# A loop over the heads, four fixed load buffers and padded queries from one masked product, in an attention kernel for one token

## The chip, the core and the metric

The kernel runs on one core of a Trainium2 chip. The metric is the time of one execution on the device in microseconds (us). The kernel before is given by the median of three runs, and one further execution was profiled.

## What is computed

One decoding step for 8 sequences. The input row of each is normalised, projected to 32 query heads of 128 numbers and attends over a cache of 8192 keys and values for each of 8 key-value heads (four query heads share one). The output projection, the input itself and a small mixer over the normalised row are added.

```
xn = _layernorm(x, axis=-1)
q = (x @ wq).reshape(B, Sq, Hq, Dh)          # x is xn here
scores = jnp.einsum("bhqd,bhkd->bhqk", q, k) * (Dh ** -0.5)
p = _softmax(scores, axis=-1)
o = jnp.einsum("bhqk,bhkd->bhqd", p, v)      # then @ wo
...
h = _layernorm(x, axis=-1)                   # mixer, x is xn
u = _gelu(jnp.einsum("bsd,sf->bdf", h, w1) + b1)
y = jnp.einsum("bdf,fs->bds", u, w2) + b2
return x + _A_ref(xn, ...) + _B_ref(xn, ...)
```

The sizes: B = 8 sequences, 8 key-value heads, 8192 keys of 128 numbers, all float32. A key tile and a value tile of one pair (head, sequence) have 4 MB each; there are 64 pairs, so 512 MB of cache, and 8 MB each of wq and wo.

## The kernel before, in words

The program is written out in full: 64 slots, one for each pair, with i = 8h + b, and the order of every engine's instructions is the order of the text (`manual_schedule`). The 4 MB tiles lie in a ring of five buffers (`ring`, name `raw`) that keys, values, wq and the last part of wo share. The order of the loads is a list: K0, K1, V0, K2, V1, K3, V2 and so on. `load_next` (L67 to L77) issues the next one on SyncE's queue. Two ring buffers are first filled with the halves of wq, and three loads stand behind them; two more are issued after the query projection has read wq. From then on `qk` (L224) and `pv` (L266) each issue one load when their last product is in the text, and the load waits until the ring buffer that it takes has been read.

A slot i goes like this:

- `qk(i)` (L228): 32 score products from the key tile and the padded queries `W`, into one PSUM bank of 128 x 512. Before it, VectorE has turned the key tile in place with four 32 x 32-block transposes (`turn`, L218). The four transposes for pair i+1 are spread over slot i.
- `sm_max`, `sm_bias`, `sm_exp` (L238, L243, L246, L252): the row maximum, its spreading over the heads by a product with the identity, a masked minimum that gives the bias, and the exponential on ScalarE, which also writes the row sums into `LR`.
- `sm_place` (L259, L261): a permuting product and a transpose that give `PT`, the weights as the value product needs them.
- `pv(i-1)` (L272): 32 value products of the pair before; `o_pick` and `o_place` (L283 to L294) gather its output.
- two steps of the mixer (L346 to L348), ScalarE's gelu and two operations of GpSimd.

At b = 0 a new head begins. The slot then also has `mx_begin` (L336, L338: a row of the normalised input spread to all partitions), `o_sums` (L311, L313), `o_scale` (L316) and `o_project` (L326, L328) of the head before. `LR`, `W` and `OTS` exist twice, for even and odd heads. `q_place` (L211) copies the queries of a whole head into the zeroed tile `W` in eight copies of 32 partitions, spread over slots 3 to 6 of the head before. `load_wo` loads 1 MB of wo for each of the first six heads in slot 2; the last two parts come behind the last value tile in a ring buffer, and `o_project(h - 1, h)` (L326) treats both heads at the end.

The last two pairs are written out by hand in an order of their own, with the last key and value tile loaded in pieces.

Of the kernel before, what the change touches and what calls it, by code (L numbers as in the profile page):

```python
# [28 lines left out]
RING = 5  # L29
PAD = 16  # L30
# [3 lines left out]
def attn_mixer_kernel(ctx: ExitStack, tc: tile.TileContext, x, kc, vc, wq, wo, w1, b1, w2, b2, out):  # L34
    nc = tc.nc
    const = ctx.enter_context(tc.tile_pool(name="const", bufs=1))
    ring = ctx.enter_context(tc.tile_pool(name="ring", bufs=RING))
# [3 lines left out]
    ps_s = ctx.enter_context(tc.tile_pool(name="ps_s", bufs=2, space=PSUM))  # L41
    ps_o = ctx.enter_context(tc.tile_pool(name="ps_o", bufs=2, space=PSUM))
    ps_h = ctx.enter_context(tc.tile_pool(name="ps_h", bufs=2, space=PSUM))
    ps_m = ctx.enter_context(tc.tile_pool(name="ps_m", bufs=2, space=PSUM))
    ctx.enter_context(tc.manual_schedule())

    def misc():
        return ps_m.tile([P, 512], F32, name="misc")
# [8 lines left out]
    order.sort(key=lambda o: o[0])  # L57
    order.reverse()
    WQ = []

    def load_wq():
        for a in range(2):
            t = ring.tile([P, NT, DH], F32, name="raw")
            t = t.rearrange("p (c n) d -> p c (n d)", c=NC // 2)
            nc.sync.dma_start(t, wq.rearrange("(p c) n -> p c n", c=NC)[:, a * NC // 2:(a + 1) * NC // 2, :])
            WQ.extend(t[:, c, :] for c in range(NC // 2))

    def load_next():
        if order:
            _, src, to, i = order.pop()  # L70
            h, b = divmod(i, B)
            t = ring.tile([P, NT, DH], F32, name="raw")
            rows = src[b, h].rearrange("(p t) d -> p t d", p=P)
            at = 0
            for n in (NT // 4,) * 4 if to is KR and i in (0, N_IT - 1) else (NT // 2, NT // 4, NT // 8, NT // 8) if not order else (NT,):
                nc.sync.dma_start(t[:, at:at + n, :], rows[:, at:at + n, :])
                at += n  # L77
            to[i] = t
        elif HKV - 1 not in wos:
            t = ring.tile([P, NT, DH], F32, name="raw")  # L80
            t = t.rearrange("p (h r c) d -> p h r (c d)", h=4, r=REP)
            for h in (HKV - 2, HKV - 1):
                rows = wo[h * REP * DH:(h + 1) * REP * DH, :].rearrange("(r p) n -> p r n", p=P)
                wos[h] = t[:, h % 2]
                for r in (slice(0, REP),) if h < HKV - 1 else (slice(0, REP - 1), slice(REP - 1, REP)):
                    nc.sync.dma_start(wos[h][:, r, :], rows[:, r, :])

    wos = {}

    def load_wo(h):  # L90
        t = one.tile([P, REP, D], F32, name="wo")
        nc.sync.dma_start(t, wo[h * REP * DH:(h + 1) * REP * DH, :].rearrange("(r p) n -> p r n", p=P))
        wos[h] = t
# [10 lines left out]
    for _ in range(RING - 2):  # L104
        load_next()
# [16 lines left out]
    nc.vector.tensor_scalar(hmask, ohw, 1.0, 3.0e38, op0=ALU.subtract, op1=ALU.mult)  # L122
# [13 lines left out]
    BO = BS * (B - 1)  # L136
    bsel = const.tile([P, BO + Q], F32, name="bsel")
    nc.vector.memset(bsel, 0.0)
    nc.vector.memset(bsel[:, BO:BO + 1], 1.0)
# [3 lines left out]
    W, OTS, LR = [], [], []  # L143
    for k in range(2):
        t = const.tile([P, B, NB, Q], F32, name=f"w{k}")
        nc.gpsimd.memset(t, 0.0)
        W.append(t)
        t = const.tile([P, REP, Q], F32, name=f"ot{k}")
        nc.vector.memset(t, 0.0)
        OTS.append(t)  # L150
        LR.append(const.tile([P, B], F32, name=f"lr{k}"))

# [25 lines left out]
    QT = const.tile([P, HKV, NB, REP, B], F32, name="qt")  # L178

    def q_project():  # L180
        hw = HKV // 2
        for a in range(2):
            m = ps_s.tile([P, 512], F32, name="s")
# [8 lines left out]
            mt = ps_o.tile([P, 512], F32, name="o")  # L192
# [9 lines left out]
            for h in range(hw):  # L202
                nc.vector.tensor_copy(QT[:, a * hw + h],
                                      mq.rearrange("p (j h x) -> p h j x", j=NB, h=hw)[:, h].rearrange("p j (r b) -> p j r b", r=REP))
        WQ.clear()

    def q_place(h, i):
        s = slice(i * Q, (i + 1) * Q)
        for k in range(2):
            o = (2 * i + k) * REP  # L210
            nc.vector.tensor_copy(W[h % 2][s, :, :, o:o + REP], QT[s, h].rearrange("p j r b -> p b j r"))  # L211

    def turn(i, a, w=NT // 4):
        if i < N_IT:
            t = KR[i][:, a:a + w, :].rearrange("p t d -> p (t d)")
            nc.vector.transpose(t, t)  # L218

    S = {}  # L220

    def qk(i):
        h, b = divmod(i, B)
        S[i] = ps_s.tile([P, 512], F32, name="s")  # L224
        kt = KR.pop(i).rearrange("p (u g) d -> p g u d", g=NG)
        for j in range(NB):
            for g in range(NG):
                nc.tensor.matmul(S[i][g * Q:(g + 1) * Q, :], W[h % 2][:, b, j, :], kt[:, g, :, j * Q:(j + 1) * Q],  # L228
                                 start=(j == 0), stop=(j == NB - 1))
        load_next()  # L230
# [3 lines left out]
    st = {}  # L234

    def sm_max(i):
        mr = work.tile([P, 1], F32, name="mr")
# [142 lines left out]
    def slot(i):  # L380
# [6 lines left out]
        if i:  # L387
            pv(i - 1)
# [85 lines left out]
```

## Time and profile before

| | |
|---|---|
| median of 3 runs | 1296.01 us (1295.83 to 1296.05) |
| the profiled execution | 1296.24 us, of which 1294.3 us lie between its first and last instruction (the span) |
| busy share of the span | TensorE 61%, VectorE 62%, ScalarE 22%, GpSimd 18% |
| moved by the DMA engines | 554.50 MB, mean 428 GB/s |
| chain of work that ended last | DMA 60%, TensorE 21%, VectorE 12%, issue 4%, ScalarE 3% |

In the rows below PE is TensorE (PEld its weight loads), DVE VectorE, ACT ScalarE, POOL GpSimd, SP SyncE, whose queue issues nearly all loads. A row of a timeline has the start in us, the duration in us, the engine, the line, the operation, the tile written and the tiles read, the shapes and the count; in square brackets stand the idle time before it and what ended that. Equal neighbours are merged into one row with their count. A row of the page's groups has the total busy time in us, the mean of one in ns, and the idle time before the group with its main cause. A row of DMA issues has the size of one and the median time in us from issue to landing.

### The profile page before, as it was taken

The page shows a single profiled execution, that of the slowest core. Times are in us where ns is not written, and L with a number is a line of the kernel's source. Part 1 is how long each engine was busy: PE and PEld are TensorE (multiplying, and loading weights), DVE is VectorE, ACT ScalarE, POOL GpSimd, SP SyncE. Part 2 cuts the span into 40 slices and gives each one's busy share as a digit, 9 for nine tenths or more (in the row PEclk, how much of TensorE's full clock was granted, in tenths as well). Part 3 has the DMA queues.
Part 4 walks back from the last instruction along what each step waited for, and adds up shares of the span by engine and source line. Part 5 has one row for each costly group of instructions (what it writes and reads, how often), then busy time and mean ns, then how long its engine had stood idle before and what let it go on. Part 6 is the DMA issues. An engine that isn't in the chain of part 4 may idle for free.

```text
span 1294.3 us, 12448 instructions
## 1 busy us (share of the span) xinstructions
PE 783.8 (61%) x5178; PEld 260.0 (20%) x5178; DVE 805.3 (62%) x834; ACT 289.4 (22%) x365; POOL 231.2 (18%) x244
## 2 busy tenths in 40 slices
PE   3376657646566556666476565575655854656657
PEld 2121112111121112211122111131111311121112
DVE  2676575575765755756656647557576566666574
ACT  0032221221212312213112222022130231213320
POOL 1022211212112111122112121121220221203310
PEclk9688777877777777787777776867868777768779
DMA  9999999999999999999999999999999999999997
GB/s 405 434 426 430 427 436 435 429 430 436 430 429 436 431 431 433 433 431 431 432 432 434 433 428 433 435 430 432 434 429 432 436 431 428 436 434 432 429 431 322
DMA packets 24491, 554.50 MB, mean 428 GB/s; under 512 B 2508, under 2 KB 2540, under 8 KB 6900
## 3 DMA queue, kind: packets, MB, share of 16 engines
q1 hardware_dynamic: 24292, 553.67, 99.5%
q8 instruction: 41, 0.67, 0.2%
q14 instruction: 14, 0.11, 0.0%
q10 hardware_dynamic: 16, 0.02, 0.0%
q0 software_dynamic: 128, 0.02, 0.0%
HBM read 553.69 MB, written 0.02 MB: 428 GB/s over the span
## 4 chain that ended last, share of the span: by engine, by line
DMA 60%; PE 21%; DVE 12%; issue 4%; ACT 3%; SPq 0%; ACTq 0%; DVEq 0%
DMA raw<-in_A_k_cache_dram 57%; DVE raw L218 10%; PE s L228 9%; PE o L272 5%; PE misc L259 3%; DMA raw<-in_A_wo_dram 2%; ACT L252 2%; DMA raw<-in_A_wq_dram 2%; DVE mr L238 1%; ACT t2k L252 1%; PE s L188 1%; PE misc L336 1%; PE misc L326 1%; PE misc L311 0%; DVE t2k L283 0%
## 5 line engine op out<-in xcount | busy, mean ns | idle before, releaser
L218 DVE STREAM_TRANSPOSE raw<-raw 128x2048 f32<-128x2048 f32 x256 | 581.9, 2293 | 346.8 <-DMA raw<-in_A_k_cache_dram 346.7
L228 PE MATMUL s<-raw,w 128*32 128x512 f32 x2048 | 315.3, 770 | 16.9 <-issue 11.8
L347 POOL TENSOR_SCALAR g<-g,w2t 128x512 f32<-128x512 f32 x112 | 77.7, 694 | 898.4 <-ACT g L346 898.4
L272 PE MATMUL o<-raw,pt 128*32 128x512 f32 x2048 | 231.4, 592 | 1.9 <-DMA raw<-in_A_v_cache_dram 1.1
L294 PE MATMUL mh<-sel,ob 128*128 128x4 f32 x126 | 35.0, 348 | 311.4 <-DVE ob L287 311.4
L252 ACT ACT_TABLE_LOAD x55 | 70.6, 1283 | 589.8 <-DVE nb L246 589.7
L348 POOL TENSOR_TENSOR macc<-macc,g 128x512 f32<-128x512 f32 x112 | 144.4, 1290 | 9.3
L259 PE MATMUL misc<-t2k,perm 128*128 128x512 f32 x128 | 124.7, 1075 | 14.4 <-ACT t2k L252 14.4
L228 PEld LDWEIGHTS s<-raw,w 128*32 128x32 f32 x2048 | 75.7, 141 | 269.0 <-issue 253.0
L346 ACT ACTIVATE g<-hb,b1t,w1t 128x512 f32<-128x512 f32 x112 | 91.0, 813 | 128.9 <-POOL macc L348 128.2
L243 PE MATMUL misc<-ident,mr 128*128 128x128 f32 x128 | 33.1, 342 | 134.0 <-DVE mr L238 134.0
L294 PEld LDWEIGHTS mh<-sel,ob 128*128 128x128 f32 x126 | 29.5, 291 | 325.4 <-DVE ob L287 324.5
L272 PEld LDWEIGHTS o<-raw,pt 128*32 128x32 f32 x2048 | 62.3, 110 | 158.1 <-issue 155.0
L252 ACT ACTIVATE t2k<-s,nb 128x512 f32<-128x512 f32 x64 | 44.0, 687 | 193.6 <-DVE nb L246 193.0
L261 DVE STREAM_TRANSPOSE pt<-misc 128x512 f32<-128x512 f32 x64 | 45.6, 712 | 42.4 <-PE misc L259 42.4
L346 ACT ACT_TABLE_LOAD x54 | 69.3, 1283 | 1.4
L243 PEld LDWEIGHTS misc<-ident,mr 128*128 128x128 f32 x128 | 20.2, 198 | 190.8 <-DVE mr L238 182.4
L238 DVE TENSOR_REDUCE mr<-s 128x1 f32<-128x512 f32 x64 | 42.1, 658 | 19.8 <-PE s L228 19.8
L283 DVE TENSOR_TENSOR t2k<-o,dm 128x512 f32<-128x512 f32 x63 | 43.1, 685 | 0.0
L211 DVE COPY w<-qt 32x128 f32<-32x128 f32 x64 | 37.0, 616 | 0.7
L259 PEld LDWEIGHTS misc<-t2k,perm 128*128 128x128 f32 x128 | 30.5, 296 | 20.3 <-ACT t2k L252 18.7
L286 DVE TENSOR_TENSOR ob<-t2k 128x256 f32<-128x256 f32 x63 | 26.8, 425 | 2.2
(75 smaller groups left out, 200.0 us busy)
## 6 DMA issues: line engine op xcount, KB each, us to landing
raw<-in_A_v_cache_dram SPq DMA_DIRECT2D x63, 4096.0 KB, 31.8
raw<-in_A_k_cache_dram SPq DMA_DIRECT2D x62, 4096.0 KB, 38.2
raw<-in_A_wq_dram SPq DMA_DIRECT2D x2, 4096.0 KB, 16.9
raw<-in_A_k_cache_dram SPq DMA_DIRECT2D x8, 1024.0 KB, 30.3
wo<-in_A_wo_dram SPq DMA_DIRECT2D x6, 1024.0 KB, 40.2
raw<-in_A_v_cache_dram SPq DMA_DIRECT2D x1, 2048.0 KB, 33.9
raw<-in_A_v_cache_dram SPq DMA_DIRECT2D x1, 1024.0 KB, 36.0
raw<-in_A_v_cache_dram SPq DMA_DIRECT2D x2, 512.0 KB, 26.8
```

Of the source, the lines that this page charges most:

```text
L218: nc.vector.transpose(t, t)
L228: nc.tensor.matmul(S[i][g * Q:(g + 1) * Q, :], W[h % 2][:, b, j, :], kt[:, g, :, j * Q:(j + 1) * Q], start=(j == 0), stop=(j == NB - 1))
L238: nc.vector.tensor_reduce(mr, S[i], AX.X, ALU.max)
L243: nc.tensor.matmul(m[:, :P], st[i].to_broadcast([P, P]), ident, start=True, stop=True)
L252: nc.scalar.activation(p, S.pop(i), AF.Exp, bias=st[i], scale=SCALE, accum_out=LR[h % 2][:, b:b + 1])
L259: nc.tensor.matmul(m, perm, st.pop(i), start=True, stop=True)
L261: nc.vector.transpose(PT[i], m)
L272: nc.tensor.matmul(O[i][c * Q:(c + 1) * Q, :], PT[i][:, u * Q:(u + 1) * Q], VR[i][:, u * NG:(u + 1) * NG, :].rearrange("p t d -> p (t d)") ...
L294: nc.tensor.matmul(MH[h][:, b * REP:(b + 1) * REP], OB.pop(i)[:, :DH], sel, start=True, stop=True)
L346: nc.scalar.activation(g, hb, AF.Gelu_apprx_tanh, bias=b1t[:, j:j + 1], scale=w1t[:, j:j + 1])
L347: nc.gpsimd.tensor_scalar(g, g, w2t[:, j:j + 1], 1.0, op0=ALU.mult, op1=ALU.mult)
L348: nc.gpsimd.tensor_add(acc, acc, g)
```

## The change

- **Loop.** Slot (0, 0) stands ahead of a loop. The loop has seven rounds; a round h holds the slots (h, 1) to (h, 7) and (h+1, 0). It has marks between stages after the slots 2, 4 and 6, and waits for the stage before on four engines after the slots 1, 3, 5 and 7. The slots (7, 1) to (7, 5) and the hand-written end follow it. There is a `prologue_barrier` ahead of slot (0, 0) and an `epilogue_barrier` at the end.
- **Buffers.** The ring becomes two key tiles and two value tiles, taken by the parity of b. wq is loaded into the two value tiles. In slot (h, b) the load of K for two pairs later stands right behind `qk(b)`, and the load of V for the next pair right behind `pv(b - 1)`. Two key loads are issued at the start, the first value load after the query projection. All other tiles and PSUM banks become fixed too, many of them single where they were double (`LR`, `OTS`, the head's output bank).
- **Queries.** `W` holds one pair instead of a head, twice. One VectorE product with a mask of zeros and ones, `imask`, writes it whole, one slot ahead.
- **Head change.** With `LR` single, `o_sums` moves ahead of `sm_exp`; `o_scale` and `o_project` move ahead of `mx_begin`, whose selecting column and that of `mx_end` are copied by two small products that read at an address from a register.
- **Smaller edits.** `sm_bias` is an addition and a minimum in place of one combined operation. GpSimd's scaling by w2 becomes a product with a broadcast; the first step of a head writes the sum directly, without the clearing and the addition. wo for the heads 0 to 6 is loaded in slot 2, and only head 7's part comes behind the last value tile.

```diff
-    KR, VR = {}, {}
-    order = []
-    for i in range(N_IT):
-        order.append((2 * i, kc, KR, i))
-        order.append((2 * i + 2.5, vc, VR, i))
...
+    K = [ring.tile([P, NT, DH], F32, name=f"k{k}") for k in range(2)]
+    V = [ring.tile([P, NT, DH], F32, name=f"v{k}") for k in range(2)]
...
+    def load(to, src, h, b, pieces=(NT,)):
+        rows = src[b, h, :, :].rearrange("(p t) d -> p t d", p=P)
+        at = 0
+        for n in pieces:
+            nc.sync.dma_start(to[b % 2][:, at:at + n, :], rows[:, at:at + n, :])
+            at += n
...
-    for _ in range(RING - 2):
-        load_next()
+    load(K, kc, 0, 0, (NT // 4,) * 4)
+    load(K, kc, 0, 1)
...
+    def q_place(h, b):
+        nc.vector.tensor_tensor(W[b % 2].rearrange("p j (x r) -> p j x r", r=REP),
+                                QT[:, h, b].unsqueeze(2).to_broadcast([P, NB, 2 * NB, REP]),
+                                imask.rearrange("p i k -> p (i k)").unsqueeze(1).unsqueeze(3).to_broadcast([P, NB, 2 * NB, REP]), ALU.mult)
...
+    def sm_bias():
         m = misc()
+        nc.tensor.matmul(m[:, :P], MR.to_broadcast([P, P]), nident, start=True, stop=True)
+        nc.vector.tensor_tensor(SQ, m[:, :P], hmask, ALU.add)
+        nc.vector.tensor_reduce(NBIAS, SQ, AX.X, ALU.min)
...
+    def mx_begin(h):
+        m = MI[2]
+        nc.vector.tensor_tensor(BM, ident[:B, bass.ds(h, 1)], ident[:B, bass.ds(h, 1)], ALU.mult)
+        nc.vector.tensor_tensor(BW, bsel[:, h, :], bsel[:, h, :], ALU.mult)
+        nc.tensor.matmul(m, BM.to_broadcast([B, P]), hn, start=True, stop=True)
+        nc.scalar.copy(HB, m)
+
+    def mx_step(j):
+        nc.scalar.activation(G, HB, AF.Gelu_apprx_tanh, bias=b1t[:, j:j + 1], scale=w1t[:, j:j + 1])
+        nc.gpsimd.tensor_tensor(G if j else ACC, G, w2t[:, j:j + 1].to_broadcast([P, D]), ALU.mult)
+        if j:
+            nc.gpsimd.tensor_add(ACC, ACC, G)
...
     q_project()
-    load_next()
-    load_next()
-    for i in range(NB):
-        q_place(0, i)
+    load(V, vc, 0, 0)
+    q_place(0, 0)
...
+    def slot(h, b, last=False, first=False):
+
+        q_place(*after(h, b, 1))
+        qk(b)
+        load(K, kc, *after(h, b, 2), (NT // 4,) * 4 if last and b == B - 3 else (NT,))
+        turn(b + 1, 0)
+        sm_max(b)
+        turn(b + 1, quart)
+        if not first:
+            pv(b - 1)
+        load(V, vc, *after(h, b, 1))
+        turn(b + 1, 2 * quart)
+        sm_bias()
+        if not first:
+            o_pick(b - 1)
+            o_place((b - 1) % B)
+        if b == 0 and not first:
+            o_sums()
+        sm_exp(b)
+        turn(b + 1, 3 * quart)
+        sm_place(b)
         if b == 0:
+            if not first:
+                o_scale()
+                o_project(wo_t)
             mx_begin(h)
...
+        for j in range(3 * b - 1, min(3 * b + 2, NF)) if last else range(2 * b, min(2 * b + 2, NF)):
+            mx_step(j)
+        if b == 2 and not last:
             load_wo(h)
+        if b == (B - 3 if last else B - 1):
+            mx_end()
...
+    tc.prologue_barrier()
+    slot(0, 0, first=True)
+    with tc.For_i(0, HKV - 1, 1, iteration_sync="staggered", head_align_engines=[nc.tensor.engine]) as h:
+        for b in range(1, B):
+            slot(h, b)
+            if b % 2:
+                for e in (nc.tensor, nc.vector, nc.scalar, nc.gpsimd):
+                    tc.previous_stage_wait(e.engine)
+            else:
+                tc.stage_boundary()
+        slot(h + 1, 0)
...
+    tc.epilogue_barrier()
```

More of the change, by code (lines that the diff above doesn't have):

```diff
@@ L121, in attn_mixer_kernel @@
     hmask = const.tile([P, P], F32, name="hmask")
[L122 removed]
+    nc.vector.tensor_scalar(hmask, ohw, 1.0, -3.0e38, op0=ALU.subtract, op1=ALU.mult)
+    nident = const.tile([P, P], F32, name="nident")
+    nc.vector.tensor_scalar(nident, ident, -SCALE, None, op0=ALU.mult)
     sel = const.tile([P, REP], F32, name="sel")
@@ L229, in qk @@
                                  start=(j == 0), stop=(j == NB - 1))
-        load_next()
-    st = {}
-    def sm_max(i):
-        mr = work.tile([P, 1], F32, name="mr")
-        nc.vector.tensor_reduce(mr, S[i], AX.X, ALU.max)
-        st[i] = mr
-    def sm_bias(i):
-        m = misc()
-        nc.tensor.matmul(m[:, :P], st[i].to_broadcast([P, P]), ident, start=True, stop=True)
-        t = one.tile([P, P], F32, name="sq")
-        nb = work.tile([P, 1], F32, name="nb")
-        nc.vector.tensor_tensor_reduce(t, m[:, :P], hmask, -SCALE, 3.0e38, ALU.add, ALU.min, nb)
-        st[i] = nb
@@ L249, in sm_exp, with sm_max @@
-    def sm_exp(i):
-        h, b = divmod(i, B)
-        p = t2k.tile([P, 512], F32, name="t2k")
-        nc.scalar.activation(p, S.pop(i), AF.Exp, bias=st[i], scale=SCALE, accum_out=LR[h % 2][:, b:b + 1])
-        st[i] = p
-    PT = {}
-    def sm_place(i):
-        m = misc()
-        nc.tensor.matmul(m, perm, st.pop(i), start=True, stop=True)
-        PT[i] = work.tile([P, 512], F32, name="pt")
-        nc.vector.transpose(PT[i], m)
-    O, MH = {}, {}
-    def pv(i, u0=0, u1=NU):
-        if u0 == 0:
-            O[i] = ps_o.tile([P, 512], F32, name="o")
+    def sm_max(b):
+        nc.vector.tensor_reduce(MR, S[b % 2], AX.X, ALU.max)
@@ L343, in mx_step @@
-    def mx_step(b, j):
-        hb, acc = mx[b]
-        g = one.tile([P, D], F32, name="g")
-        nc.scalar.activation(g, hb, AF.Gelu_apprx_tanh, bias=b1t[:, j:j + 1], scale=w1t[:, j:j + 1])
-        nc.gpsimd.tensor_scalar(g, g, w2t[:, j:j + 1], 1.0, op0=ALU.mult, op1=ALU.mult)
-        nc.gpsimd.tensor_add(acc, acc, g)
-    def mx_end(b):
-        m = misc()
+            nc.tensor.matmul(m[:, r * B:(r + 1) * B], sel[:, r:r + 1].to_broadcast([P, P]), LR, start=True, stop=True)
+        nc.vector.reciprocal(RD, m[:, :REP * B].rearrange("p (r b) -> p r b", r=REP))
@@ new lines, in attn_mixer_kernel @@
+    h = HKV - 1
+    for b in range(1, B - 2):
+        slot(h, b, last=True)
+    L = B - 1
+    q_place(h, L)
+    qk(L - 1)
+    turn(L, 0)
+    turn(L, quart)
+    sm_max(L - 1)
+    sm_bias()
+    sm_exp(L - 1)
+    turn(L, 2 * quart)
+    turn(L, 3 * quart)
+    pv(L - 2)
+    load(V, vc, h, L, (NT // 2, NT // 4, NT // 8, NT // 8))
+    load_wo_end()
+    sm_place(L - 1)
+    qk(L)
+    o_pick(L - 2)
+    o_place(L - 2)
+    sm_max(L)
+    sm_bias()
+    sm_exp(L)
+    pv(L - 1)
+    sm_place(L)
```

272 lines of the change are left out of this document (95 added, 177 removed).

## The prediction, written before the changed kernel was built or run

> **What bounds the kernel now.** I read the page first, then SyncE's, VectorE's and TensorE's timelines around the start and around a change of head, then the landing times of single loads. The first fence is from the page.
>
> ```profile
> span 1294.3 us, 12448 instructions
> ...
> DMA  9999999999999999999999999999999999999997
> ...
> q1 hardware_dynamic: 24292, 553.67, 99.5%
> q8 instruction: 41, 0.67, 0.2%
> ```
>
> The loads are the bound: in every slice but the last the 16 DMA engines are at 9 tenths or more, and the queue of the loads alone fills 99.5% of them. The change moves the same bytes. So its time is that of the stream of loads plus every microsecond in which the stream has nothing queued; nothing can win such a microsecond back. The question is how deep the queue stays. Next, SyncE's and VectorE's timelines around pair 48, the first pair of head 6.
>
> ```profile
> 990.29 0.33 SPq L76 DMA_DIRECT2D raw<-in_A_v_cache_dram  x1
> 993.73 0.33 SPq L76 DMA_DIRECT2D raw<-in_A_k_cache_dram  x1
> 1016.41 0.33 SPq L76 DMA_DIRECT2D raw<-in_A_v_cache_dram  x1
> 1019.85 0.33 SPq L76 DMA_DIRECT2D raw<-in_A_k_cache_dram  x1
> 1030.45 0.33 SPq L76 DMA_DIRECT2D raw<-in_A_v_cache_dram  x1
> ```
>
> ```profile
> 993.31 2.31 DVE L218 STREAM_TRANSPOSE raw<-raw 128x2048 f32<-128x2048 f32 x1 [6.70 <-DMA raw<-in_A_k_cache_dram]
> ...
> 1000.53 0.25 DVE L246 CUSTOM_DVE_ANT_0 sq<-misc,hmask 128x128 f32<-128x128 f32 x1
> ...
> 1012.63 2.31 DVE L218 STREAM_TRANSPOSE raw<-raw 128x2048 f32<-128x2048 f32 x1 [1.05 <-DMA raw<-in_A_k_cache_dram]
> ```
>
> The first transpose of a K tile starts when the tile has landed (its releaser is the DMA). Two K landings lie 19.32 us apart, so one load of 4 MB takes 9.66. A slot that waits for no landing is shorter: from 1016.41 to 1030.45, 14.04 us between the ends of two score products. So a slot has 5.3 us to spare, and the engines catch up after a delay; the stream can't. The edits add nothing near 5.3 us to a slot, so no engine becomes the bound.
>
> How late may a load be issued? These two answers on DMA issues (the first for the load issued at 34.70, the second over the loads of the first 60 us) and SyncE's timeline of the start give the scale.
>
> ```profile
> raw<-in_A_k_cache_dram SPq DMA_DIRECT2D x1, 4096.0 KB, 28.1
> ```
>
> ```profile
> DMA to landing us min/median/max: 12.4/25.9/39.3
> ```
>
> ```profile
> 0.74 0.87 SPq L65 DMA_DIRECT2D raw<-in_A_wq_dram  x2
> ...
> 34.70 0.33 SPq L76 DMA_DIRECT2D raw<-in_A_k_cache_dram  x1
> 35.13 0.37 SPq L76 DMA_DIRECT2D raw<-in_A_v_cache_dram  x1
> 56.20 0.33 SPq L76 DMA_DIRECT2D raw<-in_A_k_cache_dram  x1
> 73.75 0.33 SPq L76 DMA_DIRECT2D raw<-in_A_v_cache_dram  x1
> ```
>
> 12.4 us is the shortest landing time, that of the first load into an empty queue; behind others a load needs 9.66. I use 12.4 for a load that finds the queue empty (lower end: 9.66 and one us of issue, 10.7).
>
> **The change, part by part.**
>
> *Ordinary slots.* Before, five shared buffers let the load after the score product of pair i be V(i+1) and the one after its value product be K(i+3). With two buffers each, K(b+2) is issued behind the score product of b, V(b+1) behind the value product of b-1: one slot later. Call T the landing of K(b+1). Then V(b), K(b+2), V(b+1), K(b+3) follow at 9.66 each, and K(b+3) is due at T+38.6. Its issue follows the score product of b+1. In the trace such an issue came at 990.29, with T = 993.31 - 19.32 = 973.99, so at T+16.3; an empty queue would make it land at T+28.7, 9.9 us ahead of its due time. V is issued 3.4 us after it (993.73) and due 9.66 later still. So ordinary slots cost nothing: this margin of 9.9 is their cover.
>
> *The start: a hole.* Before, K2 and V1 are issued at 34.70 and 35.13 into the buffers that held wq, behind K0, K1 and V0. K2 landed at 34.70 + 28.1 = 62.8. Now wq lies in the two V buffers. At 34.70 only V0 goes out; K2 needs K0's buffer, so the first score product; and V1, whose buffer is free, stands behind K2 in SyncE's order. VectorE's and TensorE's rows there:
>
> ```profile
> 38.79 1.82 DVE L211 COPY w<-qt 32x128 f32<-32x128 f32 x8
> 40.64 11.08 DVE L218 STREAM_TRANSPOSE raw<-raw 128x2048 f32<-128x2048 f32 x5
> ```
>
> ```profile
> 49.74 6.41 PE L228 MATMUL s<-raw,w 128*32 128x512 f32 x32 [11.79 <-issue]
> ...
> 65.72 2.07 PE L336 MATMUL misc<-hn,ident 8*128 8x512 f32 x2
> 67.72 2.79 PE L228 MATMUL s<-raw,w 128*32 128x512 f32 x12
> ```
>
> The first score product ended just ahead of 56.20. Eight copies go (1.82 us) and one product of the same 128 columns comes. The page and the waits have its bounds and those of a barrier:
>
> ```profile
> L346 ACT ACTIVATE g<-hb,b1t,w1t 128x512 f32<-128x512 f32 x112 | 91.0, 813 | 128.9 <-POOL macc L348 128.2
> ...
> L348 POOL TENSOR_TENSOR macc<-macc,g 128x512 f32<-128x512 f32 x112 | 144.4, 1290 | 9.3
> ...
> L252 ACT ACTIVATE t2k<-s,nb 128x512 f32<-128x512 f32 x64 | 44.0, 687 | 193.6 <-DVE nb L246 193.0
> L261 DVE STREAM_TRANSPOSE pt<-misc 128x512 f32<-128x512 f32 x64 | 45.6, 712 | 42.4 <-PE misc L259 42.4
> ...
> L211 DVE COPY w<-qt 32x128 f32<-32x128 f32 x64 | 37.0, 616 | 0.7
> ```
>
> ```profile
> SPq L461 <- PEq L461: 0.7, 1, 0.7
> ```
>
> ```profile
> PE s L188 <- DMA raw<-in_A_wq_dram: 5.2, 1, 5.2
> ```
>
> The product lies between the 0.25 us of L246 (as many elements) and the 0.62 of L211 (scattered alike); I take 0.35. A barrier is at least the 0.7 us in which SyncE waited for the others at the launch line; at most it also waits for the loads in flight (a rival below). The issue of K2 comes at 56.20 - 1.82 + 0.35 + 0.7 = 55.4, K2 lands at 67.8, and the stream is 5.0 us late. With the lower landing time it is 3.3. The added setup on VectorE (some ten small memsets and reductions) costs nothing: the projection stood 5.2 us waiting for wq.
>
> *The change of head.* Here the order changes too. The sums are made ahead of the exponential, since the row sums now have one buffer, and the mixer's broadcast comes after the projection. TensorE's rows for this place before:
>
> ```profile
> 1002.24 0.59 PE L294 MATMUL mh<-sel,ob 128*128 128x4 f32 x2 [5.50 <-DVE ob L287]
> 1002.68 2.05 PE L259 MATMUL misc<-t2k,perm 128*128 128x512 f32 x2
> 1004.67 2.07 PE L336 MATMUL misc<-hn,ident 8*128 8x512 f32 x2
> 1006.67 1.88 PE L311 MATMUL misc<-lr,sel 128*128 128x8 f32 x8
> 1009.29 1.93 PE L326 MATMUL misc<-wo,ot 128*32 128x128 f32 x32 [0.75 <-PE misc L311]
> 1010.97 5.38 PE L228 MATMUL s<-raw,w 128*32 128x512 f32 x32
> ```
>
> With T = 993.31: the bias is two operations in place of the one at 1000.53 (0.25 us more, priced by that row), so L294 moves to 1002.5. The sums follow from 1003.0 to 1004.9. The exponential (0.69) waits for them, and the permuting product runs from 1005.8 to 1007.8. The transpose of its result (0.71) and the scaling (0.2 to 0.3) lead to the projection from 1009.2 to 1010.9; then the addition into yacc and two small products by register (0.3 each, as the 0.25 of L246), and the broadcast from 1011.9 to 1013.9. Before, the next score product stood at 1010.97, now at 1013.9. It needed 5.44 us to the issue (1016.41), so K(3) is issued at 1019.3 and lands at the latest at 1031.7, where 993.31 + 38.64 = 1031.95 is due. The margin of 9.9 is used up to 0.2 us. Here also stands the loop's back edge. Whatever it costs TensorE, call it e, the stream loses, less 0.2.
>
> The entry is alike. The broadcast at 65.72 now waits for the transpose and the two small products (1.2 us); with -0.8 from the start and 0.25 from the bias, the score product at 67.72 moves to 68.4 + e, and the issue at 73.75 to 74.4 + e. K3 then lands at 86.8 + e, against 67.8 + 2 x 9.66 = 87.1 due. At the exit nothing jumps back; I count one hand-over.
>
> *The edge e.* No row shows a jump. Below, it is the 0.7 us of one hand-over, or nothing if TensorE's queue holds work meanwhile. Code must also come in: its 41 packets took 0.2% of 16 x 1294.3 us, so about 1.0 us each. I take 0.7 + 1.0 = 1.7, so 1.5 lost, seven times (the entry and six back edges): 10.5; the exit 0.5. A round of TensorE is about 2 x 5178 / 8 = 1295 instructions.
>
> The Trainium skill (Runtime: NRT & Kernel Launch, Instruction fetch mechanics) states that a taken branch whose target is outside the two pages on hand forces a fetch of the target page before execution goes on. By that rule e is a whole fetch at every round, never hidden; without it, with TensorE's buffer holding the round, e is the hand-over alone and the sum falls by 7.
>
> *The rest.* GpSimd's scaling becomes a product with a broadcast, priced as L348: a step is 0.81 + 2 x 1.29 = 3.4 us, two of them a slot 6.8, three in the last head 10.2, within 19.3. The tail has 1 MB behind the last V piece where it had 2, and one head to project where it had two: between -1 and +1, taken as 0, with the closing barrier inside.
>
> Sum: the profiled execution's 1296.24 (span 1294.3) + 5.0 + 10.5 + 0.5 = 1312.2; it stood 0.2 over the median, so 1312.
>
> **The rivals.**
>
> *Covered edges.* TensorE's queue hides the jump, e is below 0.4, and only the start is left: 1296 + 3.3 to 5 + 1 = 1300.5 to 1302. For it: ahead of the edge TensorE waits for VectorE twice (the projection and the broadcast above), time in which its queue could take in what follows. Against: the margin of 0.2 forgives nothing.
>
> *The barriers wait for loads in flight.* At the start for V0 (62.8 - 9.66 = 53.1): the score product starts at 53.8, K2 lands at 72.7, 9.9 late. At the entry for V1 (82.4 then): K3 lands at 82.4 + 0.7 + 6 + 12.4 = 101.5, due 92.0, 9.5 late. With six edges at 1.5 and the exit: 1296 + 9.9 + 9.5 + 9.5 = 1325.
>
> *A long fetch.* A small load beside the full queue took this long:
>
> ```profile
> w1t<-in_B_w_dram POOLq DMA_DIRECT2D x1, 7.0 KB, 7.8
> ```
>
> If code waits like that, e is 8.5 and the sum 1296 + 5 + 7 x 8.3 = 1359. Against: straight-line code came in time throughout. The Trainium skill's fetch rule (the page and section above) names the same mechanism.
>
> *Not slower.* V1's buffer is free at 34.70. If SyncE's loads don't keep the written order and V1 goes out ahead of K2, the queue lasts to 62.8 and K2, landing at 67.8, is inside its 9.66 us; with an edge under 0.4 the time is 1296 to 1297. It turns on one thing: V1 issued before 53. Against: in the trace SyncE's loads stand in the written order.
>
> **How the numbers follow.** The forecast (edges of 0.5 to 4 us) has 0.48, covered edges 0.18, barriers that wait 0.17, the long fetch 0.07, not slower 0.10. The range goes from 1300, under the covered edges, to 1336, over the waiting barriers and edges of 4 us without them (1328); outside are the long fetch, not slower, and some 3 in 100 of the rest. 0.2% is 2.6 us, about what a measurement of this kernel can tell: same is 0.08, faster 0.03 (no row has 2.6 us of stream to give), slower 0.89.
>
> **What would show it.** After: SyncE's K2 at about 55.4 with V1 right behind it; slices of the DMA row below 9 at the start and about every 158 us; in each round the K issue of slot 1 some 26 to 28 us after the landing before it; ordinary slots still 19.3 us apart. K landings 19.3 us apart through the change of head would refute e; slots all longer than 19.4 would refute the whole account, since then depth, not the holes, costs.

## The result: 1.3% slower

The changed kernel takes 1313.24 us (median of 4 runs, 1310.17 to 1313.76), the kernel before 1296.03 (4 runs, 1295.83 to 1296.16): a ratio of 1.0128, with an interval of 1.0111 to 1.0146. That is 17.2 us. The profiled execution of the changed kernel is its fastest, 1310.17 us; its span is 1306.7, so 3.5 us lie outside the span where 1.9 did before.

These are the lines of the page after the change that answer to those shown of before.

```profile
span 1306.7 us, 13701 instructions
...
DMA  9999999999999999999999999999999999999998
GB/s 402 390 381 419 433 433 433 418 417 433 433 433 433 431 433 433 433 433 426 433 433 427 421 436 432 433 426 428 433 433 433 408 433 433 433 433 399 433 423 338
...
q1 hardware_dynamic: 24292, 553.67, 98.9%
q8 instruction: 12, 0.20, 0.1%
```

The same 24292 packets of loads move the same 553.67 MB. They take 98.9% of 16 engines' 1306.7 us, which is 1292.3 us for each engine; before it was 99.5% of 1294.3, 1287.8. So of the 12.4 us by which the span grew, 4.5 are load packets that took longer and the remaining 7.9 are time without a load packet (14.4 us in place of 6.5; the last digit of the share is worth 0.65 us either way). The DMA row in tenths shows none of this; the GB/s row does: slices 2 to 4, a dip about every five slices, and slice 37. The code queue has 12 packets where it had 41.

The view of busy time by windows puts a size on it. Its last two columns are the DMA share and GB/s; here are before and after, in the same four stretches: the first hole, the loop's entry, the rounds, the loop's exit.

```profile
44.00:64.00 20.00, 7.19 (x35) 2.20 (x36) 15.24 (x10) 2.06 (x3) 0.00 (x0) 0.59 1.01 436
64.00:104.00 40.00, 32.66 (x198) 9.19 (x201) 26.55 (x25) 13.44 (x16) 11.84 (x12) 0.81 1.00 432
104.00:1160.00 1056.00, 640.39 (x4039) 206.88 (x4032) 671.39 (x673) 239.67 (x299) 186.44 (x191) 0.76 1.00 432
1160.00:1200.00 40.00, 27.06 (x156) 8.58 (x155) 24.86 (x25) 14.22 (x17) 11.82 (x12) 0.76 1.00 432
```

```profile
44.00:64.00 20.00, 8.19 (x37) 2.37 (x38) 14.38 (x13) 2.06 (x3) 0.00 (x0) 0.67 0.88 362
64.00:104.00 40.00, 27.36 (x170) 7.87 (x173) 25.82 (x25) 13.32 (x16) 10.32 (x9) 0.78 0.92 392
104.00:1160.00 1056.00, 644.63 (x4062) 203.50 (x4050) 668.14 (x674) 239.01 (x298) 207.78 (x180) 0.75 1.00 430
1160.00:1200.00 40.00, 23.33 (x130) 9.10 (x134) 24.71 (x29) 8.43 (x11) 4.65 (x5) 0.67 0.95 401
```

A stretch loses its width times the missing share of the bytes. The start loses 20 x (1 - 362/436) = 3.4 us, the entry 40 x (1 - 392/432) = 3.7, the rounds 1056 x (1 - 430/432) = 4.9, the exit 40 x (1 - 401/432) = 2.9. The sum is 14.9, for a span that grew by 12.4: one unit of GB/s in the long stretch is worth 2.4 us, so its 4.9 is rough. The view of the DMA queues gives the bytes of the load queue alone for this stretch, before and after:

```profile
q1 hardware_dynamic: 18590, 455.55, 100.2%
```

```profile
q1 hardware_dynamic: 19039, 454.01, 100.1%
```

That is 1.54 MB less, or 3.6 us at 432 GB/s. The rest of the 4.9 is traffic of other queues, of code above all, that no longer comes in. With 3.6 the sum is 13.6; the other 1.2 us are won back behind 1200 us. Of all these columns only GB/s shows the loss in each of the four stretches.

**The start.** SyncE's issues after the change, and the landing of the first of these loads alone:

```profile
52.71 0.33 SPq L69 DMA_DIRECT2D k<-in_A_k_cache_dram  x1
53.09 0.42 SPq L69 DMA_DIRECT2D v<-in_A_v_cache_dram  x1
76.48 0.35 SPq L69 DMA_DIRECT2D k<-in_A_k_cache_dram  x1
79.84 0.33 SPq L69 DMA_DIRECT2D v<-in_A_v_cache_dram  x1
```

```profile
k<-in_A_k_cache_dram SPq DMA_DIRECT2D x1, 4096.0 KB, 12.8
```

K2 is issued with V1 right behind it, as forecast, at 52.71 rather than 55.4, and lands in 12.8 us: the landing time of an empty queue.

**The entry.** TensorE's rows around the loop's first score product, and ScalarE's row just ahead of it:

```profile
63.61 2.04 PE L297 MATMUL misc<-hn,bm 8*128 8x512 f32 x2 [0.93 <-DVE bw L296]
70.57 5.60 PE L226 MATMUL s<-k,w 128*32 128x512 f32 x32 [4.92 <-ACT g L301]
```

```profile
69.61 0.81 ACT L301 ACTIVATE g<-hb,b1t,w1t 128x512 f32<-128x512 f32 x1 [1.22 <-POOL macc L302]
```

TensorE has its broadcast behind it at 65.65 and then stands 4.92 us. Its score product needs nothing from the mixer, but the releaser named is the mixer's second gelu, which ends at 69.61 + 0.81 = 70.42. So at the loop's entry TensorE's first instruction waits for what ScalarE still has to do from slot (0, 0). It is the loop that does this: in e1 below, the same slots written out, this product starts at 64.92 without idle time, 2.00 us after the start of its broadcast. Which part of the loop makes it wait was not separated. K3, issued behind this product, goes out at 76.48.

**A change of head.** VectorE's, TensorE's and SyncE's rows for the first change of head inside the loop, where the back edge stands as well:

```profile
209.36 2.31 DVE L220 STREAM_TRANSPOSE k<-k 128x2048 f32<-128x2048 f32 x1 [5.96 <-DMA k<-in_A_k_cache_dram]
```

```profile
227.42 2.07 PE L297 MATMUL misc<-hn,bm 8*128 8x512 f32 x2 [0.55 <-DVE bm L295]
229.42 6.38 PE L226 MATMUL s<-k,w 128*32 128x512 f32 x32
```

```profile
236.13 0.33 SPq L69 DMA_DIRECT2D k<-in_A_k_cache_dram  x1
```

The score product behind the back edge has no bracket: it starts 2.00 us after the start of the broadcast, without idle time, as the broadcast of 2.07 us ends. It does so at all six back edges. So the back edge costs TensorE nothing. Even so K is issued 236.13 - 209.36 = 26.8 us after the landing, and by the prediction's margin (38.64 - 12.4) the queue runs dry beyond 26.2. The six changes of head inside the loop bear this out. K is issued 26.8, 25.7, 25.4, 26.9, 26.2 and 26.6 us after the landing, and in the ten microseconds around the issue (from 4 before it to 6 behind) the engines move 374, 419, 442, 406, 419 and 374 GB/s: the three late ones are the three slow ones.

What differs between the six is the length of the score product. It starts 20.1 us after the landing each time and takes 6.38, 5.32, 5.03, 6.47, 5.83 and 6.19 us, at a granted clock of 0.56, 0.68, 0.72, 0.56, 0.62 and 0.58; length times clock is 3.6 in each. So the order leaves no margin, and the granted clock of the moment decides which changes lose time. In ordinary slots K tiles go on landing 19.3 us apart (VectorE's first transposes at 132.02, 151.34 and 170.66).

**The exit.** TensorE's rows for the first score product behind the loop, and the code queue's row in the window from 1181 to 1185 us:

```profile
1179.34 2.77 PE L226 MATMUL s<-k,w 128*32 128x512 f32 x9
1184.16 3.89 PE L226 MATMUL s<-k,w 128*32 128x512 f32 x20 [2.05 <-issue]
```

```profile
q8 instruction: 1, 0.02, 1.5%
```

After nine products TensorE stops for 2.05 us, waiting for nothing that the profile shows, and a code packet comes in at this time; that TensorE waits for this packet is inferred from the time alone. The written-out e1 has the same product at the same place without a stop (5.91 us from 1178.49). The order at the change of head stands here too, so K is issued 29.3 us after its landing (1188.53 - 1159.28). In the rounds no code comes in at all. These are the queue rows for the stretch from 170 to 1180 us, first before (30 code packets), then after (the whole list: there is no q8 in it):

```profile
q1 hardware_dynamic: 17426, 435.76, 100.2%
q8 instruction: 30, 0.49, 0.2%
```

```profile
## 3 DMA queue, kind: packets, MB, share of 16 engines
q1 hardware_dynamic: 17861, 434.25, 100.1%
issues: line engine op xcount, KB each, median us to landing
```

### The profile page after: what moved, and what is told of

It is laid out like the page before. It is cut to its first block, busy times and chain, and to the rows that moved or that the text cites. A ratio compares the mean times of both kernels' runs of the same rounds, so it can differ in the third digit from the quotient of the medians.

```text
span 1306.7 us, 13701 instructions
## 1 busy us (share of the span) xinstructions
PE 788.5 (60%) x5178; PEld 257.3 (20%) x5178; DVE 814.9 (62%) x860; ACT 289.4 (22%) x365; POOL 252.3 (19%) x226
## 3 DMA queue, kind: packets, MB, share of 16 engines
q1 hardware_dynamic: 24292, 553.67, 98.9%
## 4 chain that ended last, share of the span: by engine, by line
DMA 45%; PE 24%; DVE 21%; ACT 5%; issue 1%; DVEq 0%; SPq 0%; POOL 0%; ACTq 0%
DMA k<-in_A_k_cache_dram 43%; DVE k L220 17%; PE s L226 14%; PE misc L245 5%; ACT L241 2%; DMA v<-in_A_v_cache_dram 2%; ACT pr L241 2%; DVE mr L232 1%; PE o L253 1%; PE misc L297 1%; PE misc L287 1%; PE misc L276 1%; DVE nb L238 1%; DVE sq L237 0%; DVE pt L246 0%
## 5 line engine op out<-in xcount | busy, mean ns | idle before, releaser
L220 DVE STREAM_TRANSPOSE k<-k 128x2048 f32<-128x2048 f32 x256 | 581.8, 2293 | 306.3 <-DMA k<-in_A_k_cache_dram 306.0
L226 PE MATMUL s<-k,w 128*32 128x512 f32 x2048 | 314.1, 766 | 18.1 <-DVE k L220 10.9
L253 PE MATMUL o<-v,pt 128*32 128x512 f32 x2048 | 231.9, 592 | 0.9 <-DVE pt L246 0.8
L302 POOL TENSOR_TENSOR g<-g,w2t 128x512 f32<-128x512 f32 x104 | 108.3, 1041 | 627.7 <-ACT g L301 627.7
L245 PE MATMUL misc<-pr,perm 128*128 128x512 f32 x128 | 128.2, 1104 | 23.4 <-ACT pr L241 21.2
L226 PEld LDWEIGHTS s<-k,w 128*32 128x32 f32 x2048 | 73.4, 139 | 282.3 <-issue 233.2
L236 PE MATMUL misc<-nident,mr 128*128 128x128 f32 x128 | 32.9, 341 | 113.3 <-DVE mr L232 113.3
L253 PEld LDWEIGHTS o<-v,pt 128*32 128x32 f32 x2048 | 62.0, 110 | 158.3 <-issue 156.0
L241 ACT ACTIVATE pr<-s,nb 128x512 f32<-128x512 f32 x64 | 44.0, 688 | 167.2 <-PE misc L276 147.2
L258 DVE TENSOR_TENSOR om<-o,dm 128x512 f32<-128x512 f32 x63 | 42.9, 680 | 0.0
```

The costliest lines, as they stand in the source:

```text
L226: nc.tensor.matmul(S[b % 2][g * Q:(g + 1) * Q, :], W[b % 2][:, j, :], kt[:, g, :, j * Q:(j + 1) * Q], start=(j == 0), stop=(j == NB - 1))
L236: nc.tensor.matmul(m[:, :P], MR.to_broadcast([P, P]), nident, start=True, stop=True)
L241: nc.scalar.activation(PR[b % 2], S[b % 2], AF.Exp, bias=NBIAS, scale=SCALE, accum_out=LR[:, b:b + 1])
L245: nc.tensor.matmul(m, perm, PR[b % 2], start=True, stop=True)
L253: nc.tensor.matmul(O[b % 2][c * Q:(c + 1) * Q, :], PT[b % 2][:, u * Q:(u + 1) * Q], V[b % 2][:, u * NG:(u + 1) * NG, :].rearrange("p t d - ...
L302: nc.gpsimd.tensor_tensor(G if j else ACC, G, w2t[:, j:j + 1].to_broadcast([P, D]), ALU.mult)
```

## The experiments

The theory after the result: the loss is four things in the order of the work (the start, the entry's wait, the order at a change of head, the exit), and the loop's rounds cost nothing. The rival: the loop itself, its marks and its edge, is what costs. The kernel before was run again beside them: 1296.37 us beside e1 to e4, 1296.24 beside e5 to e8 and 1296.09 beside e9 to e12. The ratios are to these runs.

**e1: no loop.** The same slots in the same order, written out, without the two barriers.

```diff
-    tc.prologue_barrier()
     slot(0, 0, first=True)
-    with tc.For_i(0, HKV - 1, 1, iteration_sync="staggered", head_align_engines=[nc.tensor.engine]) as h:
+    for h in range(HKV - 1):
         for b in range(1, B):
             slot(h, b)
-            ...
         slot(h + 1, 0)
...
-    tc.epilogue_barrier()
```

> The changed kernel with its seven rounds written out and both barriers gone; buffers, order within a slot and queries as changed. Theory (holes in the stream of loads): what is left is the start, where K2 still waits for the first score product, and the tight change of head. K2 lands about 2.9 us late as in the changed kernel, K3 follows right behind V1 because the 4.9 us wait at the loop's entry is gone, the 2 us stall behind the exit is gone: 1300 to 1303 us. Rival (two buffers each are too few: a shallower queue slows the stream everywhere, the loop costs little): 1309 to 1313 us.

Measured: 1306.71 us, ratio 1.0082 (1.0068 to 1.0096). It lies between the two forecasts. 1.8 us lie outside the span, as before: the 1.6 more belong to the loop's version with its barriers. The entry's loss is gone (64 to 104 us: 430 GB/s), the first hole is not (44 to 64 us: 387), and the rounds are as slow as after (430). So what is lost in the rounds is lost without any loop too.

**e2: no loop, three key buffers, V1 one slot earlier.** Deeper buffers should close every hole.

```diff
-    K = [ring.tile([P, NT, DH], F32, name=f"k{k}") for k in range(2)]
+    K = [ring.tile([P, NT, DH], F32, name=f"k{k}") for k in range(3)]
...
-        load(K, kc, *after(h, b, 2), (NT // 4,) * 4 if last and b == B - 3 else (NT,))
+        if i + 3 < N_IT:
+            load(K, kc, *after(h, b, 3), (NT // 4,) * 4 if i + 4 == N_IT else (NT,))
...
-PAD = 120
+PAD = 16
```

> As the run without a loop, with a third key buffer: K(i+3) is issued behind the score product of i, and K0, K1, K2, V0, V1 go out before the first score product. Theory (holes): no load waits for a product that comes too late any more, at the start or at a change of head, so the time is that of the kernel before, 1296 to 1297 us. Rival (the new order at the change of head and the single buffers slow the engines themselves): 1299 us or more, whatever the loads do.

Measured: 1304.35 us, ratio 1.0063 (1.0049 to 1.0076). The theory missed by 7 us. The queue is about as full as before the change: q1 works 99.4% of a span of 1300.6. But that is 1292.8 us for each engine, 5.0 more than before: every load is a little slower, all the way. The edit had an unnoticed side. To make room, the unused tile `pad` went from 480 to 64 bytes, and the load buffers, which begin at multiples of 4096 bytes in both kernels, then began at 48736, which is none. e5, e6 and e11 test this.

**e3: V1 ahead of K2**, with the loop.

```diff
     load(V, vc, 0, 0)
+    load(V, vc, 0, 1)
...
-        load(V, vc, *after(h, b, 1))
+        if not first:
+            load(V, vc, *after(h, b, 1))
```

> The changed kernel with V1 issued right behind V0, ahead of K2, which closes the hole before K2. Theory (the stream's place is set by the latest of its holes, not by their sum): K3 still waits for the score product behind the loop's entry, so it lands when it did, and the time stays within 1 us of the changed kernel's. Rival (holes add up): 2.5 to 3 us are won.

Measured: 1312.46 us, ratio 1.0119 (1.0103 to 1.0134): 0.8 us won. With runs from 1310.72 to 1315.55 the time alone cannot tell this from 2.5; the window rows of e3 can:

```profile
44.00:64.00 20.00, 8.24 (x36) 2.03 (x36) 14.40 (x10) 2.06 (x3) 0.00 (x0) 0.67 1.01 435
64.00:104.00 40.00, 26.24 (x154) 7.97 (x158) 25.84 (x28) 12.62 (x15) 9.38 (x9) 0.76 0.79 333
```

The first hole is closed (435) and the second has grown to 40 x (1 - 333/432) = 9.2 us, where after had 3.4 and 3.7 (e3's profiled execution, 1315.55, is its slowest, so 9.2 is rather high). K3's landing sets how late the stream is, and K3 waits for the entry. The rival (the two holes add up) falls: K3's issue follows from the engines' work and not from K2's landing, so a hole ahead of it costs nothing by itself.

**e4: the first head's mixer begun ahead of the query projection**, so that ScalarE has nothing left at the entry.

```diff
+    mx_begin(0)
+    mx_step(0)
+    mx_step(1)
     q_project()
...
-            mx_begin(h)
+            if not first:
+                mx_begin(h)
```

> The changed kernel with the first head's mixer broadcast and its two mixer steps moved ahead of the query projection, so that ScalarE and GpSimd have nothing left to do between the first exponential and the loop. Theory (TensorE's 4.9 us at the entry are a wait for ScalarE's last gelu ahead of the loop): the wait falls under 1 us, K3 is issued some 6 us sooner (the broadcast's 2 us go as well), and 3 to 5 us are won. Rival (the 4.9 us are the fetch of the loop's code): the gap at the entry stays at 3 to 5 us beyond what the broadcast took, and at most 2 us are won.

Measured: 1308.02 us, ratio 1.0095 (1.0081 to 1.011): 5.2 us won, as the theory has it. (Its runs lie between 1305.78 and 1311.08, so the size is rough, and its first hole is smaller too: 390 GB/s from 44 to 64 us, 2.1 us lost in place of 3.4.) TensorE's row at the entry now waits for VectorE's transpose alone:

```profile
63.43 5.32 PE L226 MATMUL s<-k,w 128*32 128x512 f32 x32 [0.88 <-DVE pt L246]
```

Its window from 64 to 104 us is back at 432 GB/s; the exit is not (406).

**e5: e2 with its buffers at multiples of 4096 bytes** (`PAD = 120` in place of 16, nothing else).

> The version without a loop and with three key buffers and V1 issued one slot earlier, with the load buffers moved back to addresses that are multiples of 4096 bytes (an unused tile is 416 bytes larger; nothing else differs from e2). Theory (what was left in e2, 8.0 us over the kernel before, came mostly from buffers that began at 48736 and so lay across such multiples): 1296 to 1299, with the DMA row and the packets' time as in the kernel before. Rival (the order of the work at a change of head, or the fixed buffers themselves, made it slower): 1303 to 1305 again.

Measured: 1297.77 us, ratio 1.0014 (1.0005 to 1.0023), 6.6 us under e2. The theory holds. The two rows of the stretch from 104 to 1160 us, e2 first:

```profile
104.00:1160.00 1056.00, 681.96 (x4026) 206.38 (x4022) 667.47 (x675) 238.95 (x297) 205.07 (x178) 0.80 1.00 430
```

```profile
104.00:1160.00 1056.00, 680.67 (x4050) 209.08 (x4042) 669.43 (x680) 238.95 (x297) 205.34 (x179) 0.80 1.00 432
```

The busy time of PE, DVE, ACT and POOL is the same to 0.3%; the stream differs, at a DMA share of 1.00 in both. With three key buffers, the fixed buffers and the change's order at the head cost 1.5 us in all.

**e6 and e11: the kernel before, its buffers shifted** by 32 bytes (`PAD = 24` in place of 16) and by 64 (`PAD = 32`). e6 first:

> The kernel before with its unused tile 32 bytes larger, so that the five load buffers begin 32 bytes behind multiples of 4096; nothing else. Theory (addresses lengthen the packets): 1300 to 1306. Rival (addresses do not matter): 1296 to 1296.5.

Measured: 1303.18 us (5 runs, 1303.01 to 1303.7), ratio 1.0053 (1.0039 to 1.0067): 32 bytes cost 6.9 us. Its queue row:

```profile
q1 hardware_dynamic: 24292, 553.67, 99.4%
```

That is 99.4% of a span of 1301.4, 1293.6 us for each engine, against 1287.8: 5.8 us of longer packets. For 64 bytes:

> The kernel before with its load buffers 64 bytes behind multiples of 4096 in place of 32. Theory A (what matters is a multiple of 64 bytes): 1296 to 1297. Theory B (what matters is a multiple of 512 or of 4096): 1302 to 1304, as with 32 bytes.

Measured: 1300.66 us (1300.5 to 1300.82), ratio 1.0035 (1.0021 to 1.0048): neither theory. 64 bytes cost 4.6 us, less than 32 and not nothing. What multiple is needed stays open; 4096 is enough.

**e7 and e9: the loop with all three edits of order.** V1 early as in e3, the mixer first as in e4, and the change of head as before the change: the mixer's broadcast ahead of the sums, and the sums behind the exponential, with a column `LR0` for the row sums of a head's first pair.

```diff
+    LR0 = const.tile([P, 1], F32, name="lr0")
...
-accum_out=LR[:, b:b + 1])
+accum_out=LR[:, b:b + 1] if b else LR0)
...
+        if b == 0 and not first:
+            mx_pick(h)
         qk(b)
...
-        if b == 0 and not first:
-            o_sums()
         sm_exp(b)
...
         if b == 0:
             if not first:
+                mx_begin(h)
+                o_sums()
                 o_scale()
                 o_project(wo_t)
-            mx_begin(h)
```

`mx_pick` holds the two small products that `mx_begin` had; they now stand ahead of the score product. (Slot 1 copies `LR0` into `LR`.) In e7 the new column moved the load buffers 32 bytes on; in e9 they are back (`PAD = 112`).

> The changed kernel, loop and barriers kept, with three edits of order: V1 issued with V0, the first head's mixer begun ahead of the query projection, and at a change of head the mixer's broadcast ahead of the sums and the sums behind the exponential as before the change (the first pair's row sums in a column of their own). Here the load buffers begin 32 bytes behind multiples of 4096, as in e6. Theory (the loss is the start, the entry's wait for ScalarE, the order at a change of head and the exit; the loop's back edge costs nothing): start 0 to 0.5, entry 0, heads 0 to 2, exit 2 to 3.2, 1.5 outside the span, so 1300 to 1304, plus what e6 shows for the addresses. Rival (the loop itself, its marks and its edge, costs 0.5 to 1.5 a round): 1306 to 1313.

> e7 with its load buffers back at multiples of 4096 (an unused tile 32 bytes smaller); nothing else. Theory (address and loop are separate costs; the kernel before lost 6.9 us by 32 bytes, and e7 was 9.4 us over the kernel before): 1298 to 1300, the rest being the exit and what lies outside the span. Rival (the loop's holes would have hidden the longer packets, so the two do not add): 1302 to 1305.

Measured: e7 1305.6 us, ratio 1.0073 (1.0059 to 1.0087); e9 1299.82, ratio 1.0025 (1.0016 to 1.0034). e7's expectation was 1300 to 1304 plus e6's 6.9, and it came 1.3 under that. 5.8 us lie between the two, nearly the 6.9 of the kernel before, so address and order are separate costs. e9 is 13.4 us under the changed kernel with the loop in place: the rival (the loop's marks and edge cost 0.5 to 1.5 a round) falls. Its window rows:

```profile
64.00:104.00 40.00, 27.23 (x176) 7.61 (x172) 26.63 (x27) 9.94 (x12) 7.78 (x7) 0.79 0.99 418
104.00:1160.00 1056.00, 645.50 (x4061) 205.90 (x4050) 680.91 (x692) 239.65 (x299) 207.03 (x180) 0.76 1.00 433
1160.00:1200.00 40.00, 28.94 (x181) 10.39 (x179) 24.71 (x28) 11.42 (x15) 10.30 (x9) 0.71 0.94 395
```

The rounds run at 433 GB/s, where the kernel before has 432. What is left is 1.3 us at the entry, 40 x (1 - 395/432) = 3.4 at the exit, and what lies outside the span (3.3 us, against 1.9).

**e8: the masked product alone**, in the kernel before (buffers at multiples of 4096).

```diff
-            nc.vector.tensor_copy(W[h % 2][s, :, :, o:o + REP], QT[s, h].rearrange("p j r b -> p b j r"))
+        nc.vector.tensor_tensor(W[i % 2].rearrange("p j (x r) -> p j x r", r=REP),
+                                QT[:, h, b].unsqueeze(2).to_broadcast([P, NB, 2 * NB, REP]), ..., ALU.mult)
```

> The kernel before with the masked product alone: the padded queries of one pair made by one product, one slot ahead, in place of copies of a head at a time; load buffers at multiples of 4096. Theory (VectorE has more than 5 us of room in a slot, the loads are the bound): 1295.8 to 1297. Rival (VectorE's product stands ahead of the score product and delays the issue of loads): 1298 to 1302.

Measured: 1296.35 us, ratio 1.0 (0.9991 to 1.0009). The product, with the smaller `W` and the layout of `QT` that come with it, costs nothing and wins nothing.

**e10: the order at a change of head alone**, in the changed kernel: the edits of e9 to `LR0`, `mx_pick`, `mx_begin` and `o_sums`; start and entry as changed.

> The changed kernel with the head's order alone put back: the mixer's broadcast ahead of the sums, the sums behind the exponential, the first pair's row sums in a column of their own; loop, start and entry as changed, buffers at multiples of 4096. Theory (the order at a change of head costs 1 to 3 us over the six changes and the exit, as V1's and K's issues run late there): 1309 to 1312. Rival (the order costs nothing, what is lost there is the loop's): 1313 to 1314.

Measured: 1305.26 us, ratio 1.0068 (1.0054 to 1.0082): 8.0 us won, where I expected 1 to 3. The theory names the right place and mis-sizes it; the rival falls. Start and entry are no better than in the changed kernel (366 GB/s from 44 to 64 us, 381 from 64 to 104), so all of it is won behind them. VectorE's row for the landing and SyncE's for the K issue, at the same change of head as above:

```profile
209.25 2.31 DVE L221 STREAM_TRANSPOSE k<-k 128x2048 f32<-128x2048 f32 x1 [5.62 <-DMA k<-in_A_k_cache_dram]
```

```profile
232.08 0.33 SPq L69 DMA_DIRECT2D k<-in_A_k_cache_dram  x1
```

K goes out 22.8 us after the landing in place of 26.8, on the safe side of 26.2. (Of these 4.0 us 2.0 are the order: e10's score product starts at 227.27, 18.0 after the landing, where after's starts 20.1 after. The other 1.9 are the product itself, 4.49 us in place of 6.38.) These are the window rows of the two products, after first, with the granted clock third from the end:

```profile
229.42:235.80 6.38, 6.38 (x37) 1.62 (x40) 1.65 (x1) 3.50 (x4) 2.36 (x3) 0.56 0.96 416
```

```profile
227.27:231.76 4.49, 4.49 (x42) 1.26 (x36) 3.03 (x3) 0.62 (x1) 2.33 (x2) 0.81 0.98 423
```

The product is shorter because the clock was higher, 0.81 for 0.56: length times clock is 3.6 in both. Why the clock was higher was not settled. At all six changes e10's K goes out 22.4 to 23.8 us after the landing. The window rows there and at the last change of head inside the loop, after first, then e10:

```profile
230.00:240.00 10.00, 9.65 (x66) 2.44 (x58) 5.06 (x4) 3.08 (x4) 3.36 (x3) 0.75 0.92 374
1024.00:1034.00 10.00, 7.74 (x58) 2.00 (x50) 5.80 (x6) 1.61 (x3) 3.36 (x3) 0.84 0.93 377
```

```profile
230.00:240.00 10.00, 6.22 (x57) 2.03 (x46) 9.31 (x11) 2.28 (x4) 0.38 (x1) 0.96 0.99 429
1024.00:1034.00 10.00, 6.68 (x40) 2.03 (x44) 6.24 (x9) 4.97 (x6) 3.09 (x3) 0.83 1.02 439
```

Each of these two dips costs 1.3 us, and e10 has none. Time without a load packet is not the whole of it: q1's share of e10 is 99.1% of 1300.3, 1288.6 us, so 3.7 of the 6.4 us between the two spans are packets that took longer in the changed kernel. They lie about the holes: in the first hole of the changed kernel a DMA share of 0.88 moves 362 GB/s, where before a share of 1.01 moved 436, so the same bytes took about 5% more packet time. Why was not tried.

**e12: e9 without the loop and its barriers.**

> e9 without the loop and its barriers: the same slots written out. Theory (the loop costs its exit, 2 to 3 us of TensorE standing at fresh code, and 1.5 outside the span, and nothing in its rounds): 1296 to 1298, 2 to 4 us under e9. Rival (two key and two value buffers are too few even with the order mended): 1299 to 1301 and within 1 us of e9.

Measured: 1299.01 us, ratio 1.0022 (1.0012 to 1.0031), 0.8 under e9. My theory falls: I expected 2 to 4. It has no stall at an exit, and its time outside the span is 1.8. But its rounds run at 431 GB/s against e9's 433, and its 41 code packets take their share of the engines. So what the loop gains in its rounds pays for its exit and its barriers nearly in full. The rival's number holds. e5, with a third key buffer and with the changed kernel's own order at the head, lies 1.2 us lower. Why e12's rounds, with the order mended, still lose a little was not settled.

None of these versions beats the kernel before; e8 equals it.

## Why the prediction was right, step by step

The time was forecast at 1312 and came at 1313.24, and the account behind it (the time is the stream of loads plus what the stream loses) is what the runs show, with one addition: packets can also take longer. But the terms inside the sum were off in both directions and cancelled, so that the forecast is as close as 1 us is luck. The terms can be weighed in the profiled run alone, which is the fastest of the four, 3.1 us under the median; what the other three lose beside it was not traced.

- **Ordinary slots, queries, no engine bound:** right. e9's rounds at 433 GB/s and e8's 1296.35 leave nothing for them.
- **Start, 5.0:** mis-sized; it measures 3.4. K2 went out at 52.71, not 55.4, and landed at 52.71 + 12.8 = 65.5, 2.7 us later than before. The prediction put 0.7 there for a barrier and kept the 6.41 us of the score product. TensorE's and VectorE's rows show no barrier to speak of:

```profile
47.41 5.23 PE L226 MATMUL s<-k,w 128*32 128x512 f32 x32 [10.02 <-DVE k L220]
```

```profile
38.30 0.27 DVE L212 TENSOR_TENSOR w<-qt,imask 128x128 f32<-128x128 f32 x1
```

  The product waits for VectorE's transposes alone and takes 5.23; the masked product takes 0.27 where I took 0.35.
- **Entry, 1.5:** mis-sized; 3.7 in the window, and e4 won 5.2, about 1.3 of them at the start. The step "The entry is alike" failed. Only the edge was priced there. That the loop's entry makes TensorE wait for ScalarE's gelu was not seen, though ScalarE's place (the mixer begun in slot (0, 0)) was in the diff.
- **Six back edges, 9.0:** the failing step is the price of the edge, "Below, it is the 0.7 us of one hand-over" and with the code "I take 0.7 + 1.0 = 1.7". e is 0. The Trainium skill (Runtime: NRT & Kernel Launch, Instruction fetch mechanics) says that a taken branch to a target outside the two pages on hand forces a fetch before execution goes on. By it each round would pay a fetch at its back edge; the trace shows none in the rounds, with a round of some 1295 TensorE instructions, and what looks like one at the exit, 2.05 us of standing with a code packet in it.
  What held is the step before it. The order at a change of head was worked out to use up the margin to 0.2; the K issue was to come 26 to 28 us after the landing, and it came at 26.8. But the order overshot by itself: the score product started 20.1 us after the landing, where I had 20.6, and took 6.38, where I took 5.44. The 5.44 is one product of the kernel before, which had a granted clock of 0.67; here the six took 5.03 to 6.47, at 0.72 to 0.56. The rounds lost 3.6 us against the kernel before, in place of 9.0. e10, with the loop and without this order, gains 8.0: near the 9.0 of the sum, with another cause.
- **Exit, 0.5:** mis-sized; it measures 2.9. "At the exit nothing jumps back" is true, but TensorE stops in the code behind the loop, and the late K issue of the change of head stands there too.
- **Tail and barriers, 0:** 1.6 us lie outside the span (3.5 against 1.9); every version with the loop has 3.3 to 3.5 there, and those without it 1.8 to 2.0.
- **What no term had:** longer packets about the holes (4.5 us by q1's share), and a gain: 29 code packets less. At the prediction's 1.0 us each, an estimate from a share of one digit, they are worth 29/16 = 1.8 us of the stream.

Of the rivals, covered edges had the edge right (below 0.4) and the time wrong, since it left only the start to pay. Barriers that wait for loads were wrong: the first score product started at 47.41, where that rival has 53.8. The long fetch was wrong in the rounds. Not slower was wrong twice over: V1 stayed behind K2, and e3 shows that V1 ahead of K2 would not have helped, with the entry as it is.

## What to carry to other kernels

In a kernel bound by its loads, price every edit by how late it makes the next load's issue against the landing it follows, and ask what that issue waits for. Where it follows from the engines' work and comes too late anyway, a hole ahead of it costs nothing, and mending that hole alone wins nothing (e3). Where it follows from a landing, a delay moves all that comes later, and the losses add up: e4's 5.2 and e10's 8.0 are nearly the 13.4 of e9. Here the loop's price was at its ends, in what its first instruction waits for and in the code behind the exit, and not in its rounds; an edit of order at the thinnest place cost more than the loop. A margin worked out from one product's length holds only at that product's clock. When a study changes buffers, keep their addresses, or the addresses are what is measured.

## What was not expected of the hardware

The address of a load's destination matters. With all else equal, 32 bytes off a multiple of 4096 cost the kernel before 6.9 us of 1296 (e6), 64 bytes 4.6 (e11), with the DMA share at 1.00 throughout. The Trainium skill (DMA: Bandwidth & Descriptors, How a descriptor splits into AXI transactions) says that a transfer which does not start at a multiple of 256 bytes begins at the boundary below, and that the unused bytes still cost beats, of 32 bytes each. The page speaks of bytes that are fetched; here it is the written side that is shifted. The runs agree that an unaligned start costs. They do not agree in size: by an estimate from the page, one wasted beat in the 1024 of a 32 KB piece (a 4 MB tile's part in one of 128 partitions) would be 0.1% and two 0.2%, where 32 bytes measured 0.53% and 64 bytes 0.35%, the smaller shift the dearer.

The loop's code stayed on hand: no code packet in the 1010 us from 170 to 1180, against 30 in the written-out kernel. And the granted clock of TensorE went to 0.80 in the rounds of e2 and e5 (0.75 to 0.76 elsewhere), without any gain in time: TensorE isn't the bound.
